# Strided attention feeding a gated feed-forward: a new order for the first phase, forming work split between DVE and POOL, last stores issued from two queues

## The chip, the cores and the metric

The kernel runs on one core of a Trainium2 chip. The metric is device time in microseconds for one launch, start to end; three runs of the kernel before are given. The profile is of one execution.

## The reference

```python
# q, k, v: (8 batches, 8 heads, 576 positions, 64)
scores = q @ k.T / 8                    # per batch and head
# heads 0-3: a key is seen if 0 <= i-j < 32 (local)
# heads 4-7: a key is seen if j <= i and j % 32 == i % 32 (strided)
attn = softmax(where(mask, scores, -1e9))
x    = (attn @ v) as 4608 tokens x 512
out  = (sigmoid(x @ w_gate) * (x @ w_val)) @ w_out   # 512 -> 1536 -> 512
```

Everything is float32. To keep that precision on TensorE, the kernel writes each operand as a high part in the format `fp32r` plus a low part (the operand minus its high part), and makes three matmuls out of each product: high by high, high by low, low by high.

## The kernel before

**Blocks.** The tokens are taken 512 at a time: one block of 512 for each of the eight batches, and a ninth of the 64 last tokens of every batch. The first phase does block 0 by itself, with plain products. The other eight go two at a time through four "superblocks", which multiply by a Strassen scheme of seven products P1 to P7 for each of six pairs of feed-forward chunks. It needs sums and differences of weight quarters; a set of seven operands, high and low, is called a `mix`.

**First phase.** It is written out by hand, token by token, in the string `ORDER`; each engine gets its instructions in that order and takes them strictly one after the other. It interleaves four things.

- Attention of batches 0, 1 and 2, four pairs of heads each. For pair `bp`: load (`Q`, `V`), scores on TensorE (`S`), mask, maximum and subtraction on DVE (`F`), exponential on ACT (`E`), sum and division on DVE (`N`), transposes on TensorE (`T`), copies of them on ACT (`P`), products with v on TensorE (`X`), copies to the input on ACT (`H`, `R`) and, for batch 0, the low part on DVE (`L`).
- The 36 weight pieces `f.i` (chunk `f` of 12; `i` = 0 gate, 1 value, 2 output). `W` loads a piece into one of two buffers, `first_x1h` and `first_x1l`, from SP's queue (L374); `a` and `b` (L380, L384) unpack its two halves on ACT, which frees the buffer; `w` puts them together on DVE (L393, L394); `u` casts the high part on ACT, or `U` on POOL (L404); `l` makes the low part **on POOL** (L408). After `l` of the output piece the whole piece is stored for later by a DMA **on SP's queue** (L411), the same queue on which the next `W` waits its turn.
- The products of block 0: `g` (gate and value, L416), `s` sigmoid on ACT, `m` product on DVE, `x` and `y` its high and low part (`Y`: the low part on POOL), `O` the output products (L449), `e` the stores.
- Towards the end, forming the first two mixes, `M0` and `M1`: `+` four sums (L521 to L524), `ca cd cs ct` casts of high parts on ACT (L528), `la ld ls lt` low parts (L533), `k` a store. All sums and low parts run **on POOL**. The inputs of the first superblock are formed too: `JT` differences (L349, DVE), `Jh` high parts (L359, ACT), `Jl` low parts (L361, DVE, or `JL` on POOL).

**Superblock 0.** `superblock` puts work beside the products by tick (one tick is one product, gate or value, 14 ticks to a pair of chunks). While pair `p` is multiplied, the two mixes of pair `p+1` are formed by the table `FORM`, sums and low parts on POOL. In the same ticks runs one attention step. The result of a product lies in half of a tile of two banks; ACT copies it off (L581 to L583, `gp`, `gq` and others) before a later product can use the tile.

**The end.** `store` copies four 128x512 results of the ninth block out of PSUM, by ACT and DVE in turn, and issues two DMAs for each (L463), all eight on SP's queue.

The lines are quoted by the numbers of the profile; the kernel after has them two to four lines lower.

Of the kernel before, what the change touches and what calls it, by code (L numbers as in the profile page):

```python
# [66 lines left out]
S02 b0.1 U0.0 P01 w0.1 X00 l0.0 W1.1 F02 u0.1 Z03 H00 l0.1 S03 V02 a1.0 b1.0 L00 E02 F03 g0.1.0 R00 g0.0.0 a1.1 W0.2
X01 b1.1 w1.1 E03 Q11 H01 N02 U1.1 a0.2 V03 l1.1 b0.2 L01 T02 W2.0 w0.2 R01 g0.1.1 P02 g0.0.1 Q10 w1.0 u0.2 X02 Z10
l0.2 N03 u1.0 a2.0 V10 M0+ H02 b2.0 L02 T03 w2.0 R02 S10 W2.1 P03 g0.0.2 F10 u2.0 l1.0 g0.1.2 W1.2 l2.0 g1.0.0 X03 E10
Q12 Z11 a2.1 N10 g1.1.0 H03 g1.0.1 V11 a1.2 g1.1.1 L03 b2.1 g1.0.2 b1.2 W2.2 g1.1.2 w2.1 R03 g0.1.3 g1.1.3 w1.2 U2.1  # L70
W3.0 S11 l2.1 u1.2 g0.0.3 F11 g1.0.3 Q13 a2.2 l1.2 s0 T10 b2.2 m0 g2.0 P10 W3.1 w2.2 x0 Z12 U2.2 s1 S12 a3.0 Y0 E11
g2.1 F12 Q20 l2.2 a3.1 b3.0 X10 m1 E12 W3.2 w3.0 x1 O0 H10 y1 u3.0 V12 N11 b3.1 l3.0 R10 s2 O1 W4.0 w3.1 a3.2 m2 b3.2
U3.1 g3.0 N12 x2 W4.1 l3.1 a4.0 Y2 w3.2 b4.0 T11 s3 W4.2 w4.0 U3.2 O2 P11 l3.2 a4.1 b4.1 Z13 X11 U4.0 w4.1 W5.0 a4.2
g3.1 l4.0 H11 V13 U4.1 b4.2 R11 w4.2 W5.1 l4.1 g4.0 a5.0 m3 b5.0 U4.2 x3 w5.0 W5.2 Y3 S13 s4 u5.0 l4.2 g4.1 F13 Q21
a5.1 b5.1 l5.0 a5.2 W6.0 O3 w5.1 b5.2 E13 m4 W6.1 w5.2 T12 u5.1 x4 l5.1 N13 g5.0 a6.0 P12 U5.2 y4 l5.2 b6.0 X12 a6.1
w6.0 W6.2 Z20 s5 O4 V20 b6.1 u6.0 w6.1 g5.1 H12 l6.0 a6.2 W7.0 Jh0 R12 Jl0 b6.2 S20 u6.1 W7.1 m5 g6.0 l6.1 w6.2 x5
a7.0 Q22 Y5 F20 b7.0 u6.2 g6.1 s6 l6.2 a7.1 W7.2 w7.0 b7.1 E20 O5 W8.0 m6 w7.1 x6 u7.0 y6 U7.1 T13 a7.2 N20 O6 l7.0
b7.2 P13 W8.1 l7.1 w7.2 a8.0 X13 b8.0 Z21 U7.2 w8.0 W8.2 g7.1 H13 l7.2 a8.1 V21 R13 U8.0 b8.1 S21 l8.0 w8.1 W9.0 a8.2
g7.0 b8.2 F21 u8.1 W9.1 l8.1 s7 Q23 T20 w8.2 U8.2 a9.0 g8.0 m7 a9.1 l8.2 b9.0 b9.1 w9.0 W9.2 P20 g8.1 w9.1 U9.0 W10.0
s8 Z22 E21 l9.0 S22 U9.1 g9.0 a9.2 F22 Q30 l9.1 x7 b9.2 Y7 a10.0 W10.1 X20 w9.2 E22 b10.0 O7 N22 u9.2 W10.2 H20 l9.2  # L80
R20 m8 V22 a10.1 T22 N21 x8 g9.1 b10.1 Y8 P22 W11.0 w10.1 a10.2 w10.0 O8 s9 U10.1 l10.1 u10.0 m9 b10.2 l10.0 T21 M0ca
w10.2 W11.1 g10.1 M0ct M0la M0cs u10.2 M0ls P21 g10.0 M0lt M0cd x9 a11.0 y9 Z23 l10.2 a11.1 X21 b11.0 M1+ b11.1 w11.0
W11.2 O9 s10 H21 w11.1 V23 u11.0 R21 m10 l11.0 S23 M1ca M1ct a11.2 M1lt F23 g11.0 M1cd u11.1 M1ld x10 l11.1 b11.2 X22
E23 w11.2 M1la g11.1 Y10 s11 N23 M0ld M1cs O10 m11 M0k H22 M1ls u11.2 JT1 R22 l11.2 x11 Jh1 T23 y11 Jh2 O11 JL1 P23
Jl2 X23 e0 e3 e2 e1 M1k H23 R23 JT3 Jh4 JT2 Jh5 JL4 Jh3 Jl5 Jl3 JT4 V30 Jh6 Jl6
# [7 lines left out]
def attention_then_glu(ctx, tc, qk_l, qk_s, v_l, v_s, w_all, consts, out):  # L93
# [312 lines left out]
    def lower(f, i):  # L406
        t, h, l = parts_of(f, i)
        nc.gpsimd.tensor_tensor(l, words.pop((f, i))[0].bitcast(F32), h.bitcast(F32), op=ALU.subtract)  # L408
        if i == 2:
            g, n = divmod(f, THREE)  # L410
            nc.sync.dma_start(outer[g][:, n * 2 * DM : (n + 1) * 2 * DM], t.bitcast(F32))  # L411
# [39 lines left out]
    def store(accs, b, tags, some=range(NTT)):  # L451
        for i in some:
            ob = flat(tags[i], DM, f"ob{b}_{i}")
            if i % 2:
                nc.vector.tensor_copy(ob, accs[i])  # L455
            else:
                nc.scalar.copy(ob, accs[i])
            if b is not None:
                nc.sync.dma_start(out[b * S + i * P : b * S + (i + 1) * P, :], ob)
            else:  # L460
                for n in range(P // REST):
                    at = (i * P // REST + n) * S + TB
                    nc.sync.dma_start(out[at : at + REST, :], ob[n * REST : (n + 1) * REST, :])  # L463
# [424 lines left out]
```

## Time and profile before

| | |
|---|---|
| device time, three runs | 976.62, 976.63, 978.17 us; median 976.63 |
| profiled execution | 978.2 us, of which the span from first to last instruction is 976.3 |
| PE busy | 933.0 us (96%), 7576 matmuls |
| DVE / ACT / POOL busy | 573.9 / 432.1 / 184.2 us |
| granted TensorE clock, mean | 0.982 |

PE is the engine with the most work, so time can be won where it stands idle or runs at less than its full clock. Busy time is what an instruction takes from its start to its end, and this holds any time in which it was started and then held up; idle time is put down to whatever came last before the engine went on.

### The profile page before, as it was taken

How to read it: one execution, taken by the hardware profiler on the slowest of the kernel's cores; microseconds unless marked ns; L12 is line 12 of the kernel's file. 1: busy time of each engine (PE TensorE's matmuls, PEld its weight loads, DVE VectorE, ACT ScalarE, POOL GpSimd, SP SyncE). 2: the span in 40 equal slices, each digit the busy share in tenths (PEclk: the TensorE clock that was granted, in tenths of full speed). 3: DMA queues.
4: the chain of work that ended last, by engine and by line, in shares of the span. 5: the costliest groups of instructions: out<-in, count | busy, mean ns of one | idle time of the engine just before them, and what ended most of it. 6: DMA issues, size and time to landing. Idle time of an engine off the chain costs nothing.

```text
span 976.3 us, 18003 instructions
## 1 busy us (share of the span) xinstructions
PE 933.0 (96%) x7576; PEld 749.4 (77%) x7576; DVE 573.9 (59%) x845; ACT 432.1 (44%) x773; POOL 184.2 (19%) x178
## 2 busy tenths in 40 slices
PE   5898989899999999999999999999999999999997
PEld 4677767677777778887887878888888888888885
DVE  6878778866667767466657684666355213224221
ACT  4576667666664324344454243444344223333221
POOL 1446458877771000000000000000000000000000
PEclk9799999899999999999999999999999999999999
DMA  7776673645564566956553668754625684641563
GB/s 264 255 263 223 227 275 117 273 193 211 218 243 192 182 222 229 359 199 253 223 229 118 230 233 317 287 204 168 218 112 198 233 344 179 243 182 64 194 237 108
DMA packets 43680, 212.82 MB, mean 218 GB/s; under 512 B 8656, under 2 KB 9808, under 8 KB 33360
## 3 DMA queue, kind: packets, MB, share of 16 engines
...
## 4 chain that ended last, share of the span: by engine, by line
PE 74%; DVE 10%; ACT 6%; DMA 4%; POOL 4%; issue 2%; SPq 0%; ACTq 0%; DVEq 0%; POOLq 0%
PE o L416 30%; PE o L449 12%; PE g L416 8%; PE g L449 6%; PE v L449 6%; PE v L416 6%; PE x L286 3%; PE s L191 2%; DMA first_x1h<-in_w_all 2%; POOL w L408 2%; DMA first_x1l<-in_w_all 1%; DVE pt L258 1%; POOL mix L533 1%; ACT L224 1%; DVE sb L234 1%
## 5 line engine op out<-in xcount | busy, mean ns | idle before, releaser
L449 PE MATMUL o<-wo,hs 128*128 128x512 f32 x576 | 148.3, 392 | 0.9 <-DVE ob L455 0.9
L449 PEld LDWEIGHTS o<-wo,hs 128*128 128x128 f32 x576 | 107.2, 188 | 26.7 <-DVE ob L455 2.3
L611 DVE TENSOR_TENSOR hs<-h,hs 128x512 fp32r<-128x512 f32 x96 | 63.9, 688 | 103.4 <-ACT hs L610 103.2
L568 DVE TENSOR_TENSOR h<-s,o 128x512 f32<-128x512 f32 x48 | 32.9, 685 | 97.5 <-PE o L416 92.3
L258 DVE STREAM_TRANSPOSE pt<-sb 32x320 f32<-32x320 f32 (+1 forms) x160 | 85.8, 536 | 4.9
L610 ACT CAST hs<-h 128x512 fp32r<-128x512 f32 x96 | 55.3, 618 | 74.7 <-PE o L449 47.4
L449 PE MATMUL g<-wo,hs 128*128 128x512 f32 x288 | 81.9, 393 | 0.0
L449 PE MATMUL v<-wo,hs 128*128 128x512 f32 x288 | 81.0, 389 | 0.0
L569 ACT ACTIVATE s<-s 128x512 f32<-128x512 f32 x48 | 30.4, 632 | 109.4 <-DVE s L567 109.4
L416 PE MATMUL o<-x,mix 128*128 128x512 f32 x288 | 71.9, 398 | 0.0
L416 PE MATMUL o<-x2h,mix 128*128 128x512 f32 x192 | 63.6, 392 | 3.5 <-ACT gq L583 3.5
L416 PE MATMUL o<-x3h,mix 128*128 128x512 f32 x192 | 64.2, 396 | 2.8 <-ACT o L581 2.8
L172 POOL MEMSET sb<- 128x120 f32 x10 | 2.0, 202 | 343.6 <-DVE pt L258 343.6
L416 PE MATMUL o<-x0h,mix 128*128 128x512 f32 x192 | 66.3, 406 | 0.0
L416 PEld LDWEIGHTS o<-x,mix 128*128 128x128 f32 x288 | 52.7, 188 | 16.0 <-ACT s L569 4.8
L416 PE MATMUL o<-x6h,mix 128*128 128x512 f32 x192 | 63.0, 389 | 0.0
L449 PEld LDWEIGHTS v<-wo,hs 128*128 128x128 f32 x288 | 54.1, 188 | 11.4
L449 PEld LDWEIGHTS g<-wo,hs 128*128 128x128 f32 x288 | 53.4, 188 | 11.2
L581 ACT COPY o<-o 128x512 f32<-128x512 f32 x48 | 27.4, 570 | 77.1 <-PE o L416 77.1
L228 DVE TENSOR_REDUCE mx<-sb 128x10 f32<-128x640 f32 (+1 forms) x26 | 21.3, 820 | 63.5 <-ACT sb L224 63.5
L416 PEld LDWEIGHTS o<-x2h,mix 128*128 128x128 f32 x192 | 36.0, 188 | 13.0 <-ACT gq L583 5.7
L416 PEld LDWEIGHTS o<-x3h,mix 128*128 128x128 f32 x192 | 36.7, 191 | 10.9 <-ACT o L581 3.2
...
## 6 DMA issues: line engine op xcount, KB each, us to landing
...
```

Source lines behind the costliest of these rows:

```text
L191: nc.tensor.matmul(sc[g * m : (g + 1) * m, j * BANK + s * kk : j * BANK + (s + 1) * kk], qk[d, q0 : q0 + m], qk[d, k0 : k0 + kk], start=Tr ...
L228: nc.vector.tensor_reduce(row, prob, axis=AX.X, op=ALU.add)
L258: nc.vector.transpose(dst[to : to + LB, :, col : col + LB], src[rows : rows + LB, :, h * LB : (h + 1) * LB])
L286: nc.tensor.matmul(xp[j * D : (j + 1) * D, r * BANK + (u * per + g) * m : r * BANK + (u * per + g + 1) * m], v[rows, (u * per + g) * P + j ...
L408: nc.gpsimd.tensor_tensor(l, words.pop((f, i))[0].bitcast(F32), h.bitcast(F32), op=ALU.subtract)
L416: nc.tensor.matmul(o, w, x, start=first and n == 0, stop=last and n == len(todo) - 1, skip_group_check=onto)
L449: nc.tensor.matmul(o, a[:, i * P : (i + 1) * P], b, start=first and n == 0, stop=last and n == 2)
L568: mul = lambda to, x, y: nc.vector.tensor_tensor(to, x, y, op=ALU.mult)
L569: sig = lambda to, x: nc.scalar.activation(to, x, AF.Sigmoid)
L581: run("P1", g1, v1, lambda: nc.scalar.copy(g2, g1), lambda: nc.scalar.copy(v2, v1))
L610: nc.scalar.copy(hh, src)
L611: nc.vector.tensor_tensor(hl, src, hh.bitcast(F32), op=ALU.subtract)
```

## The change

1. A new `ORDER` string of the same kinds of step. The steps `F` and `N` are now cut into their single DVE instructions, which are placed apart (`F0` mask, `F1` maximum, `F2` subtraction; `N0` sum, `N1` division). A new token `D` is `l` on DVE instead of POOL; `Mi-` is `Mi+` on DVE; `Miv.` is `Mil.` on DVE.
2. In superblock 0, the low parts of the first mix of each pair (`va vs vt vd`) go to DVE; those of the second mix and all sums stay on POOL. Their ticks are new.
3. The last block's two DMAs for each result go out on SP's and ACT's queue.

The counts by token, before and now: `l` 36, then 18 `l` and 18 `D`; `U` 17, then 10 (`u` 19, then 26); `Y` 7, then 4 (`y` 5, then 8); `JL` 2, then 0 (`Jl` 5, then 7); low parts of `M0` and `M1` on POOL 8, then 2, and 6 on DVE; sums on POOL two sets, then one, and one on DVE.

```diff
 ORDER = """
-Q00 Z00 Z01 Q01 S00 C V00 S01 F00 Q02 F01 E00 W0.0 W0.1 N00 E01 V01 a0.0 N01 T00 b0.0 Q03 P00 w0.0 T01 a0.1 Z02 W1.0
...
+Q00 Z01 Z00 V01 C S00 Q01 F000 V00 F100 F200 S01 W0.0 E00 F001 N000 W0.1 F101 N100 Q02 a0.0 F201 T00 b0.0 E01 w0.0 Q03
...
-    def lower(f, i):
+    def lower(f, i, engine=nc.gpsimd):
         t, h, l = parts_of(f, i)
-        nc.gpsimd.tensor_tensor(l, words.pop((f, i))[0].bitcast(F32), h.bitcast(F32), op=ALU.subtract)
+        engine.tensor_tensor(l, words.pop((f, i))[0].bitcast(F32), h.bitcast(F32), op=ALU.subtract)
...
-                    nc.sync.dma_start(out[at : at + REST, :], ob[n * REST : (n + 1) * REST, :])
+                    (nc.sync, nc.scalar)[n].dma_start(out[at : at + REST, :], ob[n * REST : (n + 1) * REST, :])
...
-        def sums():
+        def sums(tt=tt):
...
-        def rest_of(which):
+        def rest_of(which, tt=tt):
...
         if kind in "QVZSFENTPXHLR":
+            if len(of) == 3:
+                kind, of = kind + of[0], of[1:]
...
+        elif kind == "D":
+            lower(*map(int, of.split(".")), nc.vector)
...
+        elif what == "-":
+            room(), sums(nc.vector.tensor_tensor)
...
+        elif what[0] == "v":
+            rest_of(what[1], nc.vector.tensor_tensor)
...
-    FORM = ((0, "+"), (0, "ca"), (1, "cd"), (2, "la"), (2, "ld"), (3, "cs"), (3, "ct"), (4, "ls"), (4, "lt"), (5, "k"))
-    FORM_AT = (0, 6)
+    FORM = (
+        ((0, "+"), (0, "ca"), (1, "cd"), (2, "cs"), (2, "ct"), (3, "va"), (3, "vs"), (4, "vt"), (4, "vd"), (5, "k")),
+        ((4, "+"), (4, "ca"), (5, "cd"), (6, "la"), (6, "ld"), (8, "cs"), (8, "ct"), (9, "ls"), (9, "lt"), (10, "k")),
+    )
...
-                    for t, what in FORM:
-                        at = p * ONE + FORM_AT[i] + t
+                    for t, what in FORM[i]:
+                        at = p * ONE + t
...
+                        elif what[0] == "v":
+                            put(at, f[3], what[1], nc.vector.tensor_tensor)
```

**What moves, place 1: the last weight loads on SP's queue.** `first_x1h/l<-in_w_all` is a weight load, `outer<-w` the store of a finished output piece. Before:

```order
L374 DMA first_x1h<-in_w_all 128x1024
L411 DMA outer_79<-w_1527 128x1024
L374 DMA first_x1l<-in_w_all 128x1024
L374 DMA first_x1h<-in_w_all 128x1024
L411 DMA outer_79<-w_1719 128x1024
L374 DMA first_x1l<-in_w_all 128x1024
```

Now:

```order
L376 DMA first_x1h<-in_w_all 128x1024
L413 DMA outer_79<-w_1522 128x1024
L376 DMA first_x1l<-in_w_all 128x1024
L376 DMA first_x1h<-in_w_all 128x1024
L376 DMA first_x1l<-in_w_all 128x1024
L413 DMA outer_79<-w_1679 128x1024
```

The last load of all (`first_x1l`, piece 11.2) stood behind the store of piece 10.2 and now stands ahead of it.

**Place 2: POOL in the end stretch of the first phase,** from the last casts of chunk 10 on (`w<-whole,w` is an `l`, `mix<-` an `l` of a mix). Before:

```order
L404 CAST w_1719<-whole_1700 128x512
L408 TENSOR_TENSOR w_1719<-whole_1700,w_1719 128x512 x2
L533 TENSOR_TENSOR mix_0_0_493<-whole_214,mix_0_0_493 128x2x256
L533 TENSOR_TENSOR mix_0_0_493<-sums_0_494,mix_0_0_493 128x2x256 x2
L172 MEMSET first_x_103 128x12x10
L408 TENSOR_TENSOR w_1719<-first_x2h,w_1719 128x512
L521 TENSOR_TENSOR sums_1_1804<-whole_394 128x256
L522 TENSOR_TENSOR sums_1_1804<-sums_1_1804,whole_214 128x256
L523 TENSOR_TENSOR sums_1_1804<-whole_214,whole_394 128x256
L524 TENSOR_TENSOR sums_1_1804<-whole_214,sums_1_1804 128x256
L408 TENSOR_TENSOR w_1833<-whole_1810,w_1833 128x512
L533 TENSOR_TENSOR mix_0_1_1803<-sums_1_1804,mix_0_1_1803 128x2x256
```

Now, from the same chunk to the first sums of superblock 0:

```order
L410 TENSOR_TENSOR w_1679<-whole_1672,w_1679 128x512
L174 MEMSET first_x_101 128x12x10
L406 CAST w_1679<-first_x2h 128x512
L442 TENSOR_TENSOR first_x2l<-first_x6h,first_x2l 128x512
L410 TENSOR_TENSOR w_1810<-whole_1788,w_1810 128x512
L535 TENSOR_TENSOR mix_0_0_400<-sums_0_401,mix_0_0_400 128x2x256
L535 TENSOR_TENSOR mix_0_1_1961<-whole_206,mix_0_1_1961 128x2x256
L523 TENSOR_TENSOR sums_0_2126<-whole_680 128x256
```

Most of POOL's work of this stretch has gone. On DVE the tail after the last `y` was, before (`raw` differences, `x` low parts, `ob` copies of results):

```order
L440 TENSOR_TENSOR first_x6l<-first_x6h,first_x6l 128x512
L361 TENSOR_TENSOR x2l_1988<-raw_480,x2h_1987 128x1024
L455 COPY ob_3_2032<-o_1_838 128x512
L455 COPY ob_1_2038<-o_0_837 128x512
L349 TENSOR_TENSOR raw_1172<-raw_1172 128x1024
L349 TENSOR_TENSOR raw_480<-raw_1172,raw_480 128x1024
L361 TENSOR_TENSOR x_1_2053<-raw_1172,x_1_2053 128x1024
L361 TENSOR_TENSOR x3l_2057<-raw_480,x3h_2056 128x1024
L349 TENSOR_TENSOR raw_480<-raw_480 128x1024
```

and its last part is now, with four sums, one difference and two mix parts ahead of it:

```order
L457 COPY ob_1_1999<-o_0_735 128x512
L457 COPY ob_3_2003<-o_1_736 128x512
L363 TENSOR_TENSOR x2l_1958<-raw_484,x2h_1957 128x1024
L363 TENSOR_TENSOR x1l_2034<-raw_484,x1h_2033 128x1024
L535 TENSOR_TENSOR mix_0_1_1961<-whole_364,mix_0_1_1961 128x256
L351 TENSOR_TENSOR raw_484<-raw_1206,raw_484 128x1024
L351 TENSOR_TENSOR raw_1206<-raw_1206 128x1024
L363 TENSOR_TENSOR x3l_2054<-raw_484,x3h_2053 128x1024
L363 TENSOR_TENSOR x_1_2057<-raw_1206,x_1_2057 128x1024
L351 TENSOR_TENSOR raw_484<-raw_484 128x1024
```

DVE has taken over low parts and sums that POOL made beside it.

**Place 3: ACT in a step of superblock 0** (the second pair). Before:

```order
L528 CAST mix_2_0_2315<-whole_1015 128x256
L581 COPY o_1_2069<-o_1_2069 128x512
L317 COPY raw_2075<-x_0_2337 128x512
L325 COPY xr_2074<-x_0_2337 128x64
L582 COPY gp_1_2387<-g_2070 128x512
L528 CAST mix_2_0_2315<-sums_0_2316 128x2x256 x2
L224 ACT_TABLE_LOAD
L224 ACTIVATE sb_1_2281<-sb_1_2281 128x12x54
L582 COPY vp_1_2398<-v_2071 128x512
L583 COPY gq_1_2408<-o_0_2068 128x512
```

Now:

```order
L530 CAST mix_2_0_2315<-whole_920 128x256
L583 COPY o_1_2069<-o_1_2069 128x512
L530 CAST mix_2_0_2315<-sums_0_2316 128x2x256 x2
L319 COPY raw_2075<-x_0_2337 128x512
L327 COPY xr_2074<-x_0_2337 128x64
L584 COPY gp_1_2387<-g_2070 128x512
L226 ACT_TABLE_LOAD
L226 ACTIVATE sb_1_2281<-sb_1_2281 128x12x54
L584 COPY vp_1_2398<-v_2071 128x512
L530 CAST mix_2_1_2408<-whole_795 128x2x256
L585 COPY gq_1_2415<-o_0_2068 128x512
```

The two casts of the sums have moved from between `gp` and the exponential to before `gp`, and one cast of the second mix has moved ahead of `gq`.

More of the change, by code (lines that the diff above doesn't have):

```diff
@@ L65 @@
 ORDER = """
-Q00 Z00 Z01 Q01 S00 C V00 S01 F00 Q02 F01 E00 W0.0 W0.1 N00 E01 V01 a0.0 N01 T00 b0.0 Q03 P00 w0.0 T01 a0.1 Z02 W1.0
[L67 to L85, printed above, removed]
+Q00 Z01 Z00 V01 C S00 Q01 F000 V00 F100 F200 S01 W0.0 E00 F001 N000 W0.1 F101 N100 Q02 a0.0 F201 T00 b0.0 E01 w0.0 Q03
@@ new lines @@
+P00 N001 U0.0 a0.1 X00 Z02 N101 W1.0 b0.1 S02 w0.1 H00 T01 W1.1 L00 l0.0 u0.1 P01 F002 l0.1 g0.0.0 V02 R00 F102 a1.0
+X01 F202 Z03 b1.0 g0.1.0 H01 w1.0 S03 W0.2 a1.1 E02 F003 U1.0 b1.1 M0+ N002 Q11 F103 L01 a0.2 W2.0 g0.1.1 R01 N102
+b0.2 g0.0.1 W2.1 w1.1 T02 P02 F203 Q10 w0.2 E03 X02 Z10 u1.1 N003 l1.0 V03 a2.0 H02 N103 g1.0.0 V10 a2.1 b2.0 g1.0.1
+L02 l1.1 b2.1 T03 R02 g0.1.2 u0.2 w2.0 W1.2 g1.0.2 P03 g0.0.2 D0.2 u2.0 Z11 W2.2 X03 w2.1 g1.1.0 H03 l2.0 g1.1.1 L03
+a1.2 g1.1.2 b1.2 U2.1 V11 g0.1.3 R03 w1.2 a2.2 g0.0.3 W3.0 b2.2 g1.1.3 D2.1 s0 S11 w2.2 W3.1 g1.0.3 F011 u2.2 g2.0
@@ new lines @@
+u1.2 l2.2 m0 Q13 a3.0 F111 x0 D1.2 b3.0 g2.1 y0 a3.1 w3.0 s1 b3.1 W3.2 m1 u3.0 S10 w3.1 s2 x1 O0 W4.0 D3.0 u3.1 F010
+Y1 Q12 F110 a3.2 l3.1 g3.0 m2 b3.2 x2 w3.2 W4.1 a4.0 b4.0 F210 g3.1 s3 w4.0 W4.2 E10 F211 O1 y2 a4.1 N010 U3.2 u4.0
+b4.1 l3.2 m3 E11 W5.0 O2 N110 x3 a4.2 D4.0 b4.2 N011 Y3 W5.1 T10 w4.1 a5.0 O3 P10 N111 u4.1 Z12 w4.2 b5.0 X10 a5.1
+W5.2 w5.0 b5.1 g4.0 H10 W6.0 u4.2 D4.1 R10 D4.2 u5.0 w5.1 S12 s4 g4.1 V12 D5.0 F012 U5.1 a5.2 a6.0 l5.1 F112 b5.2 Q20
+T11 m4 b6.0 g5.0 F212 x4 P11 w6.0 W6.1 E12 Z13 y4 X11 W6.2 w5.2 O4 u6.0 H11 N012 l6.0 V13 a6.1 N112 R11 b6.1 S13 u5.2
@@ new lines @@
+W7.0 w6.1 g5.1 s5 D5.2 Q21 F013 U6.1 a6.2 g6.0 l6.1 m5 b6.2 F113 x5 W7.1 a7.0 w6.2 b7.0 T12 s6 F213 W7.2 g6.1 P12 w7.0
+E13 Z20 y5 U6.2 S20 m6 l6.2 a7.1 N013 O5 Q22 x6 F020 b7.1 Y6 F120 a7.2 W8.0 u7.0 w7.1 X12 b7.2 N113 u7.1 O6 W8.1 H12
+D7.1 Jh0 D7.0 R12 a8.0 Jl0 T13 V20 b8.0 g7.1 w7.2 P13 a8.1 Z21 w8.0 u7.2 W8.2 b8.1 X13 F220 u8.0 g7.0 w8.1 H13 V21 E20
+D8.0 W9.0 R13 u8.1 N020 l7.2 S21 s7 N120 Q23 a8.2 g8.0 F021 l8.1 b8.2 m7 a9.0 w8.2 W9.1 x7 T20 b9.0 y7 s8 g8.1 w9.0
+W9.2 P20 F121 U9.0 u8.2 Z22 F221 a9.1 X20 b9.1 D9.0 E21 W10.0 w9.1 O7 l8.2 m8 V22 H20 N021 x8 U9.1 g9.0 a9.2 N121 R20
@@ new lines @@
+b9.2 a10.0 y8 W10.1 w9.2 b10.0 S22 s9 O8 w10.0 W10.2 u9.2 F022 l9.1 u10.0 Q30 F122 a10.1 T21 M0cd D9.2 g9.1 b10.1
+D10.0 M0cs W11.0 w10.1 a10.2 M0ca M0vs u10.1 g10.0 M0va b10.2 l10.1 m9 P21 W11.1 x9 Z23 w10.2 X21 a11.0 s10 g10.1 V23
+y9 b11.0 F222 H21 W11.2 w11.0 a11.1 R21 O9 b11.1 U10.2 m10 u11.0 w11.1 x10 E22 S23 D10.2 D11.0 F023 Y10 g11.0 u11.1
+a11.2 N022 l11.1 M0ct F123 b11.2 F223 g11.1 s11 N122 w11.2 E23 T22 m11 M0lt O10 u11.2 N023 P22 D11.2 N123 x11 X22 Jh2
+y11 M1- O11 H22 R22 JT1 M1ct M1cs M1vt T23 M1ca e0 M1vs P23 e1 M1la e3 e2 X23 Jl2 Jh1 V30 M1cd Jl1 H23 M1vd R23 JT2
@@ L86 @@
+Jh4 M1k JT3 Jh3 Jl3 Jh5 Jl5 JT4 M0vd Jh6 Jl4 M0k Jl6
 """
```

## The prediction

> **What bounds the kernel now.** First the busy times by stage. The stretches are the first phase, superblock 0 up to its last forming step, and the rest; the columns are length, PE, weight loads, DVE, ACT and POOL busy, clock, DMA share and GB/s.
>
> ```profile
> 0.00:198.70 198.70, 167.60 (x2084) 131.49 (x2084) 153.87 (x203) 127.00 (x240) 110.32 (x97) 0.91 0.67 233
> 198.70:311.00 112.30, 109.69 (x1027) 86.31 (x1028) 77.94 (x118) 65.78 (x120) 72.53 (x75) 1.00 0.58 229
> 311.00:967.00 656.00, 652.92 (x4456) 529.61 (x4455) 340.67 (x523) 238.13 (x413) 1.40 (x7) 1.00 0.57 213
> ```
>
> In the 656 us after superblock 0's forming PE idles for 3; nothing that the change touches can be won there. The first phase has 31 us of idle PE and a clock of 0.91, and superblock 0 2.6. Next the waits of PE over the whole run (total, times, longest).
>
> ```profile
> PE t L245 <- DVE sb L234: 10.8, 3, 6.3
> PE g L416 <- ACT first_x6h L428: 3.6, 2, 2.0
> PE o L416 <- ACT gq L583: 3.5, 5, 0.9
> PE o L416 <- ACT o L581: 2.8, 1, 2.8
> PE x L286 <- ACT pt L268: 2.4, 1, 2.4
> PE g L416 <- POOL w L408: 2.4, 2, 2.1
> ```
>
> No wait stands out, so I followed the timeline for what lay behind the late ones. Piece 11.2 is the last weight:
>
> ```profile
> 157.24 0.69 ACT L384 ACTIVATE first_x3h<-first_x1l 128x512 int32<-128x512 uint32 x1
> 158.19 1.48 POOL L408 TENSOR_TENSOR w<-first_x2h,w 128x512 fp32r<-128x512 f32 x1
> 159.70 0.33 SPq L411 DMA_DIRECT2D outer<-w  x1
> 160.13 0.37 SPq L374 DMA_DIRECT2D first_x1l<-in_w_all  x1
> 165.12 0.67 ACT L380 ACTIVATE first_x2h<-first_x1l 128x512 f32<-128x512 f32 x1 [0.95 <-DMA first_x1l<-in_w_all]
> ...
> 106.41 0.65 ACT L384 ACTIVATE first_x3h<-first_x1l 128x512 int32<-128x512 uint32 x1
> 110.38 0.42 SPq L374 DMA_DIRECT2D first_x1l<-in_w_all  x1
> ```
>
> Its buffer is free at 157.9, yet the load leaves at 160.13: SP stands at the store of piece 10.2, which waits for POOL. Piece 7.2 lost 3.3 us the same way. Then the end stretch, from the product `m` of chunk 9 to the last `y`:
>
> ```profile
> 149.50:176.40 26.90, 24.84 (x256) 19.52 (x255) 21.83 (x24) 20.19 (x39) 26.69 (x21) 0.94 0.36 127
> ...
> 150.76 0.67 DVE L432 TENSOR_TENSOR first_x6h<-first_x6h,v 128x512 f32<-128x512 f32 x1
> ...
> 175.18 1.77 DVE L440 TENSOR_TENSOR first_x6l<-first_x6h,first_x6l 128x512 fp32r<-128x512 f32 x1
> ```
>
> POOL is busy for 26.7 of 26.9 us: here it is the bound. Last, what the two do to each other (least, median and greatest ns; the first three rows are busy us and mean):
>
> ```profile
> L393 DVE TENSOR_SCALAR first_x2h<-first_x2h 128x512 int32<-128x512 int32 x12 | 9.1, 759 | 0.4 <-ACT first_x2h L380 0.4
> L393 DVE TENSOR_SCALAR first_x3l<-first_x3l 128x512 int32<-128x512 int32 x12 | 8.8, 737 | 0.1
> L393 DVE TENSOR_SCALAR first_x3h<-first_x3h 128x512 int32<-128x512 int32 x12 | 7.2, 597 | 3.6 <-ACT first_x3h L380 3.6
> ...
> L393 DVE TENSOR_SCALAR first_x3h<-first_x3h x12: 411/420/1652, 15.9 to 156.9; 128x512 int32<-128x512 int32 x12
> ...
> L232 DVE TENSOR_SCALAR mx<-mx x7: 173/717/1283, 12.6 to 198.6; 128x10 f32<-128x10 f32 x7
> ...
> L408 POOL TENSOR_TENSOR w<-whole,w x24: 1262/1296/1875, 18.0 to 167.4; 128x512 fp32r<-128x512 f32 x24
> ...
> L440 DVE TENSOR_TENSOR first_x6l<-first_x6h,first_x6l x3: 685/699/1769, 62.4 to 175.2; 128x512 fp32r<-128x512 f32 x3
> ```
>
> The 128x10 instruction needs 0.17 us and takes up to 1.28, one POOL instruction longer. A low part is 0.69 us on DVE, 1.26 on POOL, and on either may be stretched by the other's length. The 36 L393 alone hold 25.1 - 36 x 0.411 = 10.3 us of such holding.
>
> **The change part by part.** The sum is made in differences against the profiled execution (976.3 span, 978.2 with what lies around it; 1.6 above the median of 976.63) and set against the median.
>
> *Work moved, first phase.* POOL loses 18 `l`, 3 `Y`, 6 mix parts, a set of sums, two `JL` and 7 casts and keeps about 18 x 1.27 + 8 two-input instructions of 1.27 + 10 casts of 0.65 + two sets of sums of 3 = 46 us, from 110. DVE gains 18 + 3 low parts and 4 wide mix parts at 0.69, two narrow ones and four sums at about 0.4 (estimate, half of 0.69 and a little), two `Jl` at 1.24: 22 us. L393 shows 10.3 us of holding, the 13 divisions of L232's kind some 7 at their median; if holding falls with POOL's load, to 46/110, these two give back 10. DVE thus rises from 154 to at most 166 us and, since others are held too, more likely stays near 155. In itself this is worth nothing; the order decides.
>
> *Weight loads.* In the new order 7.2 and 11.2 leave ahead of the store. 7.2: 3.3 us on one of two buffers, half of it if the other goes on, so -1.5 (0 to -3.3). 11.2 counts in the next term.
>
> *End stretch.* From that product of chunk 9 to the end of the last `y` it is 176.95 - 150.76 = 26.2 us now. DVE's instructions between the same two in the new order come to 17.4 us (four `w` of 1.11, seven low parts at 0.69, two sums of rows, two divisions and one mask-to-subtraction at the 0.82 of their rows, and so on), and POOL's five to six two-input instructions may hold it for 1.26 each. The other path is ACT's: from the first unpacking of the last piece, eight more instructions of about 0.57 and two table loads of 1.28 lead to the last `y`, some 8.4 us, against 176.95 - 165.12 = 11.8 now. Either way the stretch is 20 to 23 us: I take -4.5 (0 to -8.8).
>
> *From the last `y` to product P6 of superblock 0.*
>
> ```profile
> 193.34 0.79 PE L416 MATMUL o<-x3h,mix 128*128 128x512 f32 x1 [2.80 <-ACT o L581]
> ...
> L361 DVE TENSOR_TENSOR x6l<-raw,x6h x1: 1239/1239/1239, 192.3 to 192.3; 128x1024 fp32r<-128x1024 f32 x1
> ```
>
> Now 193.34 - 176.95 = 16.4 us. In the new order DVE has sums (1.6), two wide and two narrow mix parts, three differences, two copies and six `Jl` behind `y`, of which 16 us precede the high part of x6; ACT's cast of 1.05 and its copy for P6 follow: 17.7. The last transposes are no longer followed by the output products of chunk 11, so PE waits for ACT's copies there too. I take +1.5 (-2.8, if the wait shown vanishes, to +4).
>
> *Clock.* The same twelve matmuls, behind the wait of 2.4 us and elsewhere:
>
> ```profile
> 95.95 5.26 PE L449 MATMUL o<-w,first_x2l 128*128 128x512 f32 x12
> ...
> 148.33 2.89 PE L449 MATMUL o<-w,first_x2l 128*128 128x512 f32 x12
> ```
>
> A wait of some 2 us can thus cost 2.4 more. Which are left I can't read from an order; I take -1 (two such stretches fewer, -5, to one more and a bit, +3). The Trainium skill (TensorE: Matmul & The Clock Gate, Part 1, the two states) has the clock halved after at least one idle window of about 3.4 us; by that rule waits of 2.4 would cost nothing beyond themselves, this term would be 0 and the sum 1 us less. The row speaks against it, and the measurement decides.
>
> *Superblock 0.* ACT and PE in one step:
>
> ```profile
> 216.86 0.59 ACT L582 COPY gp<-g 128x512 f32<-128x512 f32 x1 [0.88 <-PE g L416]
> 217.34 1.14 ACT L528 CAST mix<-sums 128x512 fp32r<-128x512 f32 x2
> 218.50 1.28 ACT L224 ACT_TABLE_LOAD   x1
> 220.92 0.58 ACT L583 COPY gq<-o 128x512 f32<-128x512 f32 x1
> 221.55 0.50 PE L416 MATMUL o<-x2h,mix 128*128 128x512 f32 x1 [0.65 <-ACT gq L583]
> ...
> 220.58 0.83 DVE L228 TENSOR_REDUCE mx<-sb 128x12 f32<-128x648 f32 x1 [5.16 <-ACT sb L224]
> ```
>
> Without the two casts (1.16 from start to next start) and with one wide cast (about 0.55) ahead of it, `gq` comes 0.6 us sooner and the wait of 0.65 goes in four steps; in the first, the table for the exponential is already there (it followed another exponential), and 0.9 goes. The new DVE work, 3 x 0.69 + 0.4 = 2.5 us, fits in the 5.16 that DVE waits there. Against it: the second mix's sums now wait until DVE has read the first's, and a late sum holds ACT. Of the 3.5 I take -2.5 (-3.5 to +3.5).
>
> *Last stores.*
>
> ```profile
> 968.44 5.02 SPq L463 DMA_DIRECT2D out<-obNone  x8
> 969.87 0.69 DVE L455 COPY obNone<-v 128x512 f32<-128x512 f32 x1 [0.67 <-PE v L449]
> ...
> L463 SPq DMA_DIRECT2D out<-obNone x8: 540/565/602, 968.4 to 972.9; - x8
> ...
> DMA to landing us min/median/max: 2.3/2.3/2.4
> ```
>
> Eight issues at 5.02/8 = 0.63 us end at 973.46. With two queues, the last result is ready at 970.56; ACT, behind DVE's second copy and its own DMA, copies `g` some 0.7 us later, and both queues end near 971.75: -1.7 (-0.6, if each issue is dearer on ACT, to -2.2).
>
> Sum: -1.5 - 4.5 + 1.5 - 1 - 2.5 - 1.7 = -9.7; 976.63 - 9.7 = 966.9.
>
> **The rivals.**
>
> *DVE becomes the bound (slower).* PE, ACT and POOL would all wait for one engine that has got 22 us more. The place is the first phase; it decides where holding gives back less than 22 - 4 us, since superblock 0 and the stores bring about 4. At the 10 us of the two rows above, the phase is 12 us longer and the time 976.6 + 12 - 4 = 984.6; at 14 given back, 980.6. For it: DVE is busy 77% now, takes its work in order and feeds each `u` and `l`. Against: the waits named above end on POOL, ACT and a DMA, only the first (mostly at the start of the run) on DVE. The Trainium skill (SBUF — State Buffer, section on the shared port pair) says that a DVE instruction with two SBUF inputs and a POOL instruction that reads SBUF block each other fully; by that rule the moved instructions are of the contending kind on either engine, which is this rival.
>
> *The order is worth nothing.* The phase ends where it did, its gains eaten by waits elsewhere; superblock 0 and the stores remain: 976.6 - 4.2 = 972.4. For it: 31 us of idle PE come from many short waits, and an order only shifts them.
>
> *Nothing.* The joint (+4) and a cold stretch (+2.4) take back all that is left of the rest: about 976.
>
> *More.* If the end stretch runs at DVE's 17.4 us, two cold stretches go and most of the 10.8 us wait at the start shrinks by 3: -8.8 - 5 - 3 - 4.2 = -21, 955.6.
>
> **How the numbers follow.** A measurement of this kernel tells about 0.2%, 2 us, from no change. Forecast (a gain of 6 to 15 us): 0.54. Order worth nothing: 0.15. More: 0.10. These make faster 0.79. Nothing: 0.10. DVE the bound: 0.11. The forecast's own range is 961.5 to 970.5. The range to hold the time 8 times in 10 is 956 to 976.5: it leaves out the DVE rival and the last of the "more" and "nothing" cases. The worst ends of the terms sum to +10, the best to -26.
>
> **What would show it.** Right: the first product of superblock 0 starts 5 to 8 us earlier; POOL's busy time in the phase is near 46 us, DVE's near 155, with L393 near 0.5 us on average; the load of the last piece leaves within 0.1 us of its buffer's release; PE's wait for `gq` is below 1 us in all; the last issue ends 1.7 us sooner after the last matmul. Wrong: DVE's busy time in the phase above 165 with PE waiting for its rows; new waits of PE at the last transposes and at P6 beyond 4 us in all; ACT standing at a cast of sums in superblock 0.

## The result and the profile after

The kernel after takes 961.97 us (median of 4 runs, 958.43 to 963.21) against 976.62 of the kernel before (4 runs, 974.40 to 978.17): ratio 0.9846, 95% interval 0.9813 to 0.9879, or 14.65 us less. Forecast were 9.7. The profiled execution took 962.69, its span is 960.9 (976.3 before). On another chip the same kernel took 958.89 us, so each kernel below is compared with runs on its own chip.

The stages of the kernel after, with the same columns as in the prediction. The first three lines answer to its first three. The last three divide the first phase after 60 us at the product `m` of chunk 9, the end of the last `y`, and P6.

```profile
0.00:181.31 181.31, 154.44 (x2084) 121.98 (x2085) 154.34 (x239) 130.79 (x248) 50.62 (x53) 0.98 0.74 255
...
181.31:294.00 112.69, 112.17 (x1032) 88.99 (x1033) 85.80 (x136) 66.03 (x121) 53.56 (x59) 0.98 0.59 230
294.00:953.00 659.00, 655.08 (x4452) 528.82 (x4451) 340.24 (x523) 236.96 (x410) 1.39 (x7) 1.00 0.56 212
...
60.00:138.98 78.98, 78.65 (x946) 62.81 (x945) 68.25 (x108) 63.88 (x116) 20.33 (x20) 1.00 0.77 257
138.98:158.40 19.42, 19.23 (x218) 14.80 (x218) 18.70 (x31) 17.26 (x32) 6.35 (x6) 1.00 0.41 143
158.40:176.09 17.69, 11.72 (x199) 9.36 (x191) 17.19 (x21) 11.54 (x24) 7.62 (x5) 1.00 0.66 243
```

And of the kernel before, the stretch that answers to the fourth line:

```profile
60.00:150.76 90.76, 84.62 (x870) 66.77 (x869) 73.41 (x98) 60.48 (x110) 47.35 (x42) 0.94 0.72 244
```

P2 of superblock 0 starts at 181.31 instead of 198.71: 17.4 us are won in the first phase. From 60 us to the last `y` PE now idles for 0.5 of 98.4 us, at clock 1.00. Before, 8.2 of 117 were idle, at 0.94 and 0.93. The two stretches do not hold the same work, since the new order is further on at 60 us: the product `m` of chunk 2 starts at 58.1 us, where before that of chunk 1 started at 60.6. Over the whole phase the work is the same: its 2084 matmuls keep PE busy for 154.4 us instead of 167.6, and PE idles for 26.9 us instead of 31.1. So 13.2 of the 17.4 us are busy time of PE, and 4.2 are idle time. Behind 294 us there is nothing to win, as forecast; something is lost there, which is taken up below.

PE's longest waits, over the whole run (total, times, longest):

```profile
PE t L247 <- DVE sb L236: 3.7, 1, 3.7
PE o L418 <- ACT o L583: 3.2, 1, 3.2
...
PE g L418 <- ACT first_x6h L430: 2.4, 2, 2.0
PE o L418 <- ACT gq L585: 2.2, 1, 2.2
```

The 10.8 us at the transposes have shrunk to 3.7, and the 2.4 for POOL's `w` are gone. Of the waits for `gq` four are gone and the first has grown from 0.9 to 2.2.

What the path goes through between 60 and 140 us (the chain of waits of that window, shares by line), before and after:

```profile
by line: DMA first_x1l<-in_w_all 17.8%; DMA first_x1h<-in_w_all 15.0%; POOL w L408 9.5%; issue 6.0%; PE g L416 5.7%; ACT first_x2h L380 3.9%; PE v L416 3.5%; ACT first_x2h L384 2.8%; DVE first_x2h L393 2.2%; DVE sb L217 2.2%; DVE sb L234 2.
```

```profile
by line: PE o L451 21.6%; PE v L418 17.9%; DMA first_x1h<-in_w_all 15.2%; PE g L418 13.4%; PE x L288 5.7%; PE s L193 3.5%; PE t L247 2.7%; ACT w L406 2.1%; ACT L430 2.0%; issue 1.9%; ACT first_x3l L386 1.6%; ACT first_x2h L382 1.6%; ACT fir
```

Before it went through a bit of everything, weight loads first. Now more than half of it is PE's own products.

The rows that answer to the prediction's steps: the last weight (buffer freed, loaded, unpacked) with the store that stood ahead of its load, then the product of chunk 9, the last `y`, P6 and P2.

```profile
142.21 0.68 ACT L386 ACTIVATE first_x3h<-first_x1l 128x512 int32<-128x512 uint32 x1
142.91 0.33 SPq L376 DMA_DIRECT2D first_x1l<-in_w_all  x1
146.79 0.33 SPq L413 DMA_DIRECT2D outer<-w  x1
148.88 0.67 ACT L382 ACTIVATE first_x2h<-first_x1l 128x512 f32<-128x512 f32 x1
...
138.98 0.68 DVE L434 TENSOR_TENSOR first_x6h<-first_x6h,v 128x512 f32<-128x512 f32 x1
157.72 0.68 DVE L442 TENSOR_TENSOR first_x6l<-first_x6h,first_x6l 128x512 fp32r<-128x512 f32 x1
176.09 0.50 PE L418 MATMUL o<-x3h,mix 128*128 128x512 f32 x1 [3.21 <-ACT o L583]
181.31 0.61 PE L418 MATMUL o<-x2h,mix 128*128 128x512 f32 x1 [2.19 <-ACT gq L585]
```

The span's 15.4 us in places, before against after: up to the product of chunk 9, 150.76 to 138.98: -11.8. From there to the end of the last `y`, 26.19 to 19.42: -6.8. To P6, 16.39 to 17.69: +1.3. To P2, 5.37 to 5.22: -0.2. From P2 to the last matmul's start, 770.73 to 773.84: +3.1. From there to the end, 6.86 to 5.75: -1.1.

The start has its own row. SP's queue, before and after, up to the first weight load:

```profile
5.99 0.33 SPq L161 DMA_DIRECT2D qk<-in_qk_l  x1
6.36 0.43 SPq L374 DMA_DIRECT2D first_x1h<-in_w_all  x1
```

```profile
2.61 0.43 SPq L167 DMA_DIRECT2D vv<-in_v_l  x1
3.08 0.45 SPq L376 DMA_DIRECT2D first_x1h<-in_w_all  x1
6.14 0.33 SPq L163 DMA_DIRECT2D qk<-in_qk_l  x1
```

The first weight stood behind a load of `qk` that waited for its buffer until 5.99. In the new order it leaves at 3.08. This alone is not the gain, for the fifth load leaves at 23.18 us before and at 23.45 after. The lead comes behind it; the ninth load, before and after:

```profile
46.32 0.33 SPq L374 DMA_DIRECT2D first_x1h<-in_w_all  x1
```

```profile
38.98 0.42 SPq L376 DMA_DIRECT2D first_x1h<-in_w_all  x1
```

The thirteenth leaves at 52.52 instead of 64.2.

The end, answering to the prediction's rows of the last stores:

```profile
954.15 3.22 SPq L465 DMA_DIRECT2D out<-obNone  x4
954.16 1.46 ACTq L465 DMA_DIRECT2D out<-obNone  x2
...
955.58 0.69 DVE L457 COPY obNone<-v 128x512 f32<-128x512 f32 x1 [0.67 <-PE v L451]
955.65 0.58 ACT L459 COPY obNone<-g 128x512 f32<-128x512 f32 x1 [1.53 <-PE v L451]
956.27 1.38 ACTq L465 DMA_DIRECT2D out<-obNone  x2
...
DMA to landing us min/median/max: 2.4/2.7/3.0
```

SP's four issues do not follow back to back: from 955.44 to 956.26 SP waits for ACT's copy of `g`.

And how long instructions of L395 (L393 before) are held (busy us, mean ns):

```profile
L395 DVE TENSOR_SCALAR first_x3l<-first_x3l 128x512 int32<-128x512 int32 x12 | 6.7, 557 | 0.2 <-ACT first_x3l L382 0.2
...
L395 DVE TENSOR_SCALAR first_x3h<-first_x3h 128x512 int32<-128x512 int32 x12 | 5.9, 489 | 1.3 <-ACT first_x3h L382 1.3
L395 DVE TENSOR_SCALAR first_x2h<-first_x2h 128x512 int32<-128x512 int32 x12 | 5.7, 476 | 1.9 <-ACT first_x2h L382 1.9
```

The 36 take 18.3 us instead of 25.1, 0.51 on average.

### The profile page after: what moved, and what is told of

Its sections match the earlier page's. It is cut to its first block, busy times and chain, and to the rows that moved or that the text cites. A ratio compares the mean times of both kernels' runs of the same rounds, so it can differ in the third digit from the quotient of the medians.

```text
span 960.9 us, 18012 instructions
## 1 busy us (share of the span) xinstructions
PE 924.2 (96%) x7576; PEld 741.5 (77%) x7576; DVE 581.8 (61%) x898; ACT 435.0 (45%) x780; POOL 105.6 (11%) x118
## 4 chain that ended last, share of the span: by engine, by line
PE 79%; DVE 10%; ACT 5%; DMA 3%; issue 1%; SPq 0%; ACTq 0%; DVEq 0%
PE o L418 31%; PE o L451 14%; PE g L418 8%; PE v L418 8%; PE g L451 6%; PE v L451 6%; PE x L288 3%; PE s L193 2%; DMA first_x1h<-in_w_all 2%; DVE pt L260 1%; DMA wo<-outer 1%; DVE hs L613 1%; ACT L226 1%; DMA first_x<-in_qk_s 1%; ACT mix L530 1%
## 5 line engine op out<-in xcount | busy, mean ns | idle before, releaser
L451 PEld LDWEIGHTS g<-wo,hs 128*128 128x128 f32 x288 | 53.4, 188 | 11.2
L571 ACT ACTIVATE s<-o 128x512 f32<-128x512 f32 x48 | 28.7, 597 | 37.6 <-PE o L418 37.5
```

What stands on the lines that cost most here:

```text
L451: nc.tensor.matmul(o, a[:, i * P : (i + 1) * P], b, start=first and n == 0, stop=last and n == 2)
L571: sig = lambda to, x: nc.scalar.activation(to, x, AF.Sigmoid)
```

## The experiments

Each kernel was timed against the kernel before on the same chip (its medians there: 975.72, 975.30 and 975.53 us), and ratios are to it. Three theories were at stake: A, POOL was the bound and the split frees it; B, the sequence of the steps takes out PE's waits; C, the two load buffers of the weights set the pace.

**The parts behind the first phase, and order and split apart.** Three kernels, all with the new forming table and the new stores.

```diff
 later_parts
-ORDER = (the new string)
+ORDER = (the old string)
 sequence_alone: the new string, each work on its old engine
-... D0.2 ... M0vs ... M1- ... Jl1 ...
+... l0.2 ... M0ls ... M1+ ... JL1 ...
 engines_alone: the old string, each work on its new engine
-... l0.2 ... M0ls ... M1+ ... JL1 ...
+... D0.2 ... M0vs ... M1- ... Jl1 ...
```

> The old first phase, with the new forming table of superblock 0 and the last stores on two queues. The prediction's terms for these two are -2.5 and -1.7, so 972.4 us against 976.6. The profile of the kernel after speaks for less: the products between the first wait for gq and the end of superblock 0's forming gained 0.8 us there, the end about 1.1, so 974.7. P2 of superblock 0 should start near 198.7 us as before, less 0.9 if its wait for gq goes.

> The new sequence of steps, but each piece of work on the engine that had it before (all 36 low parts of weights, the low parts and sums of the mixes, the two JL and the same casts on POOL as before). Theory A, that POOL was the bound and the split over DVE and POOL frees it: most of the gain is lost, 971 to 975 us, P2 at 194 to 198. Theory B, that the sequence takes out PE's waits and the cold stretches behind them: most of it stays, 963 to 966 us, P2 at 181 to 185. If the sequence only fits the new split, it is slower than before, above 980.

> The old sequence, with each piece of work on the engine that has it now. Theory A: most of the gain stays, 963 to 967 us, P2 near 183 to 187. Theory B: 971 to 975 us. The prediction's rival that DVE becomes the bound: P2 5 us or more later than 198.7 and the time above 978.

Measured: `later_parts` 970.90 us, ratio 0.9949 (0.9933 to 0.9966); `sequence_alone` 967.18, 0.9914 (0.9891 to 0.9936); `engines_alone` 971.88, 0.9958 (0.9940 to 0.9975). The profiles, in us, by the same four places (the kernel after was profiled again in the next group):

| kernel | product of chunk 9 | to the last y | to P6 | to P2 | P2 at |
|---|---|---|---|---|---|
| before | 150.8 | 26.2 | 16.4 | 5.4 | 198.7 |
| later_parts (old, old) | 146.5 | 26.2 | 16.4 | 5.9 | 194.9 |
| engines_alone | 145.6 | 27.3 | 15.4 | 5.9 | 194.2 |
| sequence_alone | 137.5 | 22.7 | 22.3 | 5.2 | 187.8 |
| after | 139.0 | 19.4 | 17.7 | 5.2 | 181.3 |
| after, again | 134.8 | 20.6 | 17.7 | 5.2 | 178.2 |

Executions differ by some 4 us up to chunk 9; the later stretches repeat within about 1. The product of chunk 9 comes at 147.6 us on average in the three profiles of the old sequence above, and at 136.8 in the six of the new one (these three, and the three kernels of the next group): 10.8 us by the sequence, on either set of engines. The profiles of the two groups do not overlap (145.6 to 150.8, and 134.8 to 139.0). What the split does there does not stand out. So A falls up to chunk 9, and B holds as far as it names the sequence; which of its moves bring the time is open. In the last two stretches the two belong together. The old sequence gives 42.6 us on the old engines and 42.7 on the new. The new one gives 45.0 on the old and 37.1 to 38.2 on the new. The same stretches of `sequence_alone`:

```profile
137.53:160.24 22.71, 21.48 (x244) 16.59 (x242) 21.15 (x26) 18.35 (x34) 16.52 (x14) 1.00 0.43 152
160.24:182.57 22.33, 13.10 (x166) 10.22 (x164) 15.82 (x11) 11.16 (x24) 19.98 (x13) 0.81 0.74 271
```

Behind the last `y` POOL is busy for 20.0 of 22.3 us with work that the new sequence had put late on DVE, and PE waits 4.9 us at P6. In the old sequence the split is worth nothing: 971.88 us against 970.90. By the medians the sequence alone gives 3.7 us (967.18), and it would be about 7 without a loss of 3.4 behind the first phase that comes with the new string (it is taken up below). `sequence_alone` lies between the times expected by A and by B; without this loss it would be at about 963.8, within B's 963 to 966. The split pays where the new sequence crowds work.

`later_parts` comes to 4.8 us; the prediction had 4.2 for it, and the profile of the kernel after had spoken for 1.9.

**One part of the change taken back.** Four kernels on one chip, the kernel after among them.

```diff
 addresses_back
-Q00 Z01 Z00 V01 C ...
+Q00 Z00 Z01 V01 C ...
 form_back: FORM and FORM_AT as in the kernel before
 stores_back
-(nc.sync, nc.scalar)[n].dma_start(out[...], ob[...])
+nc.sync.dma_start(out[...], ob[...])
```

> The kernel after, unchanged, as the standard for the kernels that undo one part of it: 961 to 963 us. If the late products whose moving operand is x (x4 and x5) belong to the kernel and not to one execution, some 9 in 10 of them again follow at a pitch of 0.233 us instead of 0.227.

> The kernel after with the old forming table of superblock 0 (all low parts and sums on POOL, the second mix six ticks behind the first). By the prediction's term it loses 2.5 us: 964.5, with PE's waits for gq back in most steps. By the profile of the kernel after, where superblock 0 gained 0.8 us behind P2: 963. If the two casts were what held gq in the steps, the waits of 0.65 are back at each of the four later ones.

> The kernel after with the last eight stores on SP's queue alone. By the prediction's term it loses 1.7 us: 963.7; by the ends of the two profiles (5.7 us and 4.6 us behind the last copy) 1.1 us: 963.1. The eight issues should again follow at 0.63 us and end some 3.6 us behind the last matmul's end.

> The kernel after with Z00 written ahead of Z01, which moves no instruction of PE, DVE, ACT or SP and only gives the tiles x5 and x4 their places in SBUF as in the kernel before (28512 and 36704 bytes, 96 more than a multiple of 128, instead of 25376 and 33568, 32 more). If these places make the products of x4 and x5 follow at 0.233 us: some 450 of 560 products gain 0.0065 us each, 2.9 us, so 959 us with a count of slow ones near the 75 of before. If the slow pitch comes from something else: as the kernel after, 961 to 963 us, with 520 of 560 slow.

Measured: `after_again` 958.89 us (958.45 to 959.86), ratio 0.9831 (0.9809 to 0.9853); `form_back` 961.25 (959.73 to 964.13), 0.9856 (0.9833 to 0.9878); `stores_back` 959.79 (959.54 to 961.18), 0.9842 (0.9820 to 0.9864); `addresses_back` 955.49 (954.92 to 956.01), 0.9795 (0.9773 to 0.9817). The intervals against the kernel before overlap for the first three, so the 2.4 us of the forming and the 0.9 of the stores rest on medians and profiles; the runs of `addresses_back` all lie below those of `after_again`. The standard came out 2 us below the 961 to 963 expected, and with it the other three, so only the differences can be compared with what was expected.

`form_back` has the waits back, 1.8 us at the first and 0.65 at each of the four later ones:

```profile
PE o L418 <- ACT gq L585: 4.4, 5, 1.8
```

Now the loss behind the first phase. What the prediction did not see: the new order also gives some tiles new places in SBUF. A tile gets its place when a step first names it, and the new string names Z01 ahead of Z00 (`Z` reserves the tiles of a pair and clears a part of one on POOL). This puts x5 and x4 at bytes 25376 and 33568 instead of 28512 and 36704. Products whose moving operand is one of these, between 800 and 930 us (busy us, mean ns of one): in the kernel before, in the kernel after, and in `addresses_back`:

```profile
L416 PE MATMUL g<-x,mix 128*128 128x512 f32 x36 | 9.1, 389 | 0.0
```

```profile
L418 PE MATMUL g<-x,mix 128*128 128x512 f32 x30 | 7.8, 394 | 0.0
```

```profile
L417 PE MATMUL g<-x,mix 128*128 128x512 f32 x30 | 7.6, 389 | 0.0
```

Busy time over count is 0.260 in the kernel after and 0.253 in the other two. By the starts of one matmul and the next, 522 of 560 products of this kind follow at about 0.233 us in the kernel after, 524 of 561 in its second profile, 66 of 557 in `addresses_back` and 75 of 546 before; the others at 0.227. The kernels with the old string have few slow ones (65 of 561 in `later_parts`, 103 of 561 in `engines_alone`); `sequence_alone`, with the new one, has 517 of 560. With them go products of x6: 86 of 273 follow at 0.231 us or more in the kernel after, none before and none in `addresses_back`. The edit moves no instruction of PE, DVE, ACT or SP, and gives 3.4 us. The slow products account for about that: some 540 fewer at 0.0065 us each are 3.5 us (an estimate from these counts).

**Old sequence, with the loads or the clock mended.**

```diff
 stream (the kernel before; likewise for all 36 pieces)
-... W1.0 ... a0.0 N01 T00 b0.0 ...
+... a0.0 b0.0 W1.0 N01 T00 ...
 keep_warm (the kernel before): 10, 8, 8 more matmuls at K
+... g5.0 K10 ... T20 K8 ... S23 K8 ...
+nc.tensor.matmul(acc[0][0], zero, xs0["h", 0], start=False, stop=False)
```

> The kernel before with two kinds of step moved and nothing else: each b (the second half's unpacking, which frees the buffer) right behind its a on ACT, and each load W right behind the b that frees its buffer, so ahead of the stores on SP's queue. If the cycle of the two load buffers sets the first phase (time of the last a = first issue + half the sum over all pieces of lateness, flight and unpacking: 17.2 + 217.8 + 78.0 us in the kernel before, 4.4 + 227.1 + 57.9 in the kernel after): lateness to about 5 and unpacking to about 46 take 22 us from the sum; with some 8 us given back to longer flight, the last a comes 14 us sooner (151 instead of 165) and the time is 964 to 969 us, as far as POOL can follow. If the loads matter only where the prediction saw them (pieces 7.2 and 11.2): 974 us. If POOL was the bound: the last a comes sooner but P2 does not, 975 to 977.

> The kernel before with 10, 8 and 8 more matmuls of a zero operand (added to block 0's output sums, which they do not change) just ahead of three waits of PE, near 91, 125 and 162 us; it is extra work that fills the waits. If what the cold stretches cost counts (the twelve matmuls behind the first at 0.43 us each, 4.6 us in the three places): the stretches at 96, 128 and 166 us go, and the time is 973 to 975. If PE's speed there is hidden behind the weights' stream: the stretches go and the time stays, 975 to 977.

Measured: `stream` 974.02 us, ratio 0.9976 (0.9961 to 0.9991); `keep_warm` 976.94, 1.0014 (1.0002 to 1.0025).

In `stream` the sum of lateness falls from 17.2 to 5.5 us and that of unpacking from 78.0 to 44.6, as wished. But the time from a load's issue to its unpacking grows from 217.8 to 254.4: buffers come free sooner, the pieces arrive sooner, and lie there until ACT's order comes to them. The unpacking of the last piece starts at 160.3, against 161.4 in `later_parts` and 145.1 to 148.9 in the kernel after. C falls as the cause of the large gain. What prompt loads of all 36 pieces are worth in the old sequence, 2.3 us (0.9 to 3.8), is near the 1.5 that the prediction gave piece 7.2.

In `keep_warm` the group of twelve behind the second wait ran like this:

```profile
123.64 2.11 PE L649 MATMUL o<-xh,zero 128*128 128x512 f32 x8
...
125.58 0.39 PE L417 MATMUL g<-xh,w 128*128 128x512 f32 x1
...
128.30 0.39 PE L417 MATMUL v<-xh,w 128*128 128x512 f32 x1
```

The group takes 2.72 us; in the kernel before the same one took 4.42, from 127.27 to 131.69. Two of the three cold stretches are gone, the first only moved (to 102.6). The time is not shorter, and P2 starts at 194.8 us, as in the other profiles of the old sequence in this part (194.2 to 195.0; the 198.7 of the kernel before is the latest of the five). In the old sequence PE's lower rate in these places was hidden behind the waits of others. Up to P2's first products, 46 matmuls of 512 columns follow at about 0.43 us instead of 0.235 in the kernel before and 21 in the kernel after, which is about 9 us against 4. By `keep_warm` this is a sign that PE waits less, not a cause of the gain in itself; the cold stretches that `keep_warm` did not fill were not tried.

**Towards a better version.**

```diff
 second_mix_on_pool (the kernel after)
-... M0lt ... Jh2 y11 M1- ... M1ct M1cs M1vt ... M1vs ... M1vd ... Jl3 Jh5 Jl5 JT4 M0vd
+... M0lt M0ld M1+ ... Jh2 M1ct M1cs y11 ... M1lt M1ls ... M1ld ... Jl3 JT4 Jh5 Jl5
 best (the kernel after, places as in addresses_back)
-... Jl3 Jh5 Jl5 JT4 M0vd Jh6 Jl4 M0k Jl6
+... Jl3 JT4 Jh5 Jl5 Jh6 Jl4 Jl6 M0vd M0k
-    at = p * ONE + t
+    at = p * ONE + t + (p == 0)
 best_on_128
+pad = flat("pad", 8, "pad")
```

> The kernel after, with the sums and low parts of the second mix (and the last low part of the first) back on POOL, which stands idle there for 10 us twice, and with the last difference of inputs ahead of a low part that is not needed yet. DVE loses 1.6 + 1.3 + 0.4 + 0.4 = 3.7 us of its chain between the last y and P6, and the cast of x6 comes 1.2 us sooner. If DVE's own work is the bound there: P6 starts 3 to 5 us sooner against P1's beginning of the phase (about 172 instead of 176.1), and the time is 958 to 959.5. If POOL's instructions hold DVE's up by as much: no change, 961 to 963.

> The kernel after with the tiles x5 and x4 at their old places (3.4 us measured), the last difference of inputs one low part sooner (the cast of x6 1.2 us sooner), the last low part of the first mix behind the inputs (0.4 us), and superblock 0's forming of the second pair's mixes one tick later, so that ACT's casts no longer stand ahead of its copies for P6 and P2 (0.5 us). P6 about 1.6 us sooner than with the places alone: 954 us if 955.5 is the standard, ratio to before 0.978. If the waits only pass to P2 (its copy stands behind the exponential): 955.5, ratio 0.9795.

> The same with a tile of 32 bytes ahead of all others, which moves every tile to a multiple of 128 bytes instead of 96 more than one. If a place 32 bytes off is what makes a product slow and 96 is no worse than 0: no change against the kernel without it. If an operand that straddles such a border costs at 96 as well in some places (x0 and x1 show 116 slow of 360 products): these go to 0.227 and 0.7 us is won.

Measured: `second_mix_on_pool` 961.59 us, ratio 0.9848 (0.9827 to 0.9870), no better than the kernel after. `best` 956.24, 0.9808 (0.9791 to 0.9824), and `best_on_128` 955.97, 0.9799 (0.9785 to 0.9813), both no better than `addresses_back`.

In `second_mix_on_pool` DVE has lost 3.7 us of work between the last `y` and P6, but the cast of x6 comes only 2.0 us sooner behind `y` (13.6 instead of 15.6), the stretch is 2.0 shorter (15.7), and the one before it 0.9 to 2.1 longer than in the kernel after's two profiles. What POOL got back, it takes while DVE works:

```profile
160.36 2.33 DVE L362 TENSOR_TENSOR x2l<-raw,x2h 128x1024 fp32r<-128x1024 f32 x1
...
160.35 1.26 POOL L534 TENSOR_TENSOR mix<-whole,mix 128x512 fp32r<-128x512 f32 x1
```

The DVE instruction takes 1.22 us in the kernel after; beside POOL's 1.26 it takes 2.33. The kernel after has such holding too, but less of it. Beside POOL's sums two of its differences take 1.76 us, one without POOL 1.22:

```profile
167.03 1.76 DVE L351 TENSOR_TENSOR raw<-raw,raw 128x1024 f32<-128x1024 f32 x1
...
172.74 1.22 DVE L351 TENSOR_TENSOR raw<-raw 128x1024 f32<-128x1024 f32 x1
```

In `best` P6 does start sooner behind the last `y`, 16.1 instead of 17.7 us, but PE then waits 3.3 us for `gq`, where the kernel after waits 2.2 (the copy stands behind the exponential, which waits for DVE), and P2 starts at 178.4, against 178.8 in `addresses_back`. The wait only passed on. The best of the kernels measured is thus the kernel after with Z00 ahead of Z01: 955.49 us.

## Why the prediction came out as it did

The forecast, a gain of 6 to 15 us, is what happened. The sum came there by errors of both signs. Of the signs of being right, the last load, DVE's busy time and L395's mean came as named. Others did not: the first product of superblock 0 starts 16.5 us earlier (167.14 instead of 183.64), not 5 to 8, and PE waits 2.2 us for `gq`, where less than 1 was named.

- **Weight loads, -1.5.** The load of the last piece leaves 0.02 us behind its buffer's release (142.89), as foretold, and making all loads prompt in the old sequence gives 2.3. The mechanism was right; the 1.5 for piece 7.2 was not measured by itself.
- **What the sum lacked: about 10 us up to the product of chunk 9.** This is the step that failed. The prediction priced the named waits of the first phase and took it that outside of them the phase would stay; its rival even said that an order only shifts short waits. As for idle time the rival was nearly right: of the 31.1 us that PE idled in the phase 26.9 are left, but now nearly all before 60 us and behind the last `y`. What the sequence took out is mostly busy time: from 60 us to the last `y` PE works almost without a wait (0.5 us) and at clock 1.00, and the phase's matmuls take 13.2 us less. The first row of the prediction, 167.6 us of PE at clock 0.91 in 198.7, had this room in it.
- **End stretch, -4.5, 20 to 23 us.** 19.4 in the profile compared, 20.6 in the second. The direction and nearly the size were right, the floor was not: PE is busy for 19.2 of the 19.4 us, so PE's own work fills the stretch, and DVE's 17.4 us are not its floor.
- **Last `y` to P6, +1.5.** 17.69 us against 17.7 forecast. The count of DVE's instructions behind `y` was the right view: the difference that the cast of x6 waits for ends 15.6 us behind `y`, where 16 were forecast.
- **Clock, -1.** Eight cold stretches became three, but `keep_warm` shows for two of the old ones that they were hidden. Which wait brings a cold stretch can't be told from its length. P6 comes after a wait of 3.21 us both in the kernel after and in `addresses_back`; it follows at near full rate in the kernel after (176.09 to 178.74 for eleven steps), and at 0.43 us a step in `addresses_back`. P2 comes after one of 2.19 us in the first profile of the kernel after and of 2.20 in the second; it starts at 0.43 us a step in the first, and runs at near full rate in the second. (The rows stand below the list.) The Trainium skill (TensorE: Matmul & The Clock Gate, Part 1, the two states) halves the clock after at least one idle window of about 3.4 us; the slow start behind 2.19 us disagrees with that read as one wait, as the row in the prediction did.
- **Superblock 0, -2.5.** `form_back` loses 2.4. The four later waits for `gq` are gone, but the first is 2.2 us instead of none: there the copy stands behind an exponential that waits 0.64 us for DVE, and behind a cast of 0.62.
- **Stores, -1.7.** About 1 (0.9 in `stores_back`; 1.1 by the ends of the profiles). The issues came out nearly as forecast: the last one ends 2.50 us behind the start of the last matmul instead of 4.02, 1.5 us sooner. Mis-sized was the landing: the last store takes 3.0 us from its issue instead of 2.4 (medians 2.7 and 2.3). ACT also gets to its copy of `g` only when its own two issues are out.
- **DVE the bound.** DVE's busy time is 154.3 us (155 forecast), POOL's 50.6 (46), and L395's mean is 0.51 (0.5). DVE got an estimated 22 us of work and is busy no longer than before (153.9); the instructions of L395 alone give 6.8 of it back. So this rival did not come. The Trainium skill (SBUF — State Buffer, Who interferes with whom) says that a DVE instruction with two SBUF inputs contends with a POOL instruction that reads SBUF; the rows of `second_mix_on_pool` agree (2.33 us instead of 1.22). It cost there, where POOL was loaded again, and less in the kernel after, where POOL does less.
- **Places in SBUF, +3.4.** Not in the prediction at all. Without them the time would have been near 958.5, outside the forecast's own range of 961.5 to 970.5 and inside the range given. That the time lies in the forecast's own range, 0.5 us from its end, is luck.

The rows of the two waits that the result does not show, P6 in `addresses_back` and P2 in the second profile of the kernel after:

```profile
173.54 0.80 PE L417 MATMUL o<-x3h,mix 128*128 128x512 f32 x1 [3.21 <-ACT o L582]
```

```profile
178.20 0.50 PE L418 MATMUL o<-x2h,mix 128*128 128x512 f32 x1 [2.20 <-ACT gq L585]
```

With the values from the profiles: -11.8 - 6.8 + 1.3 - 0.2 + 3.1 - 1.1 = -15.5, the difference of the spans but for rounding. The +3.1 holds the gain in superblock 0 (about 0.8), the loss by places (3.4) and a wait of PE for a DMA that the profile before does not have:

```profile
749.80 1.62 PE L451 MATMUL o<-wo,hs 128*128 128x512 f32 x6 [0.86 <-DMA wo<-outer]
```

Why this wait came is open.

Open: which of the moves up to chunk 9 bring how much. The earlier first load and the shorter waits at the first transposes are seen, but were not tried one by one. The lead of the weights' stream arises between the fifth load and the thirteenth, from 23 to 64 us of the kernel before, so that is where to look. `stream` shows that it is not the handling of the load buffers.
